# A Fourier-mixing and gated-FFN kernel on one Trainium2 core: a reordered opening, earlier x loads and earlier layer-2 work

## The chip, the cores and the metric

The kernel runs on one core of one Trainium2 chip. The metric is device time in microseconds (us) of one execution. Each timed kernel ran beside the kernel before on the same chip, in the same rounds.

The engines are called by the names that the profile uses: PE (matrix multiplication), PEld (its weight loads), ACT (activation functions and copies), DVE (vector work), POOL (a second vector engine, which here also issues some DMAs) and SP (which issues the other DMAs). A "q" behind a name, as in SPq, means the engine's instruction queue, that is the time to issue something. Batches, chunks and blocks are counted from 0.

## The reference

A Fourier transform along the tokens and one along the channels, of which the real part goes into a gated feed-forward layer:

```python
def _attn_ref(x):                       # x: 8 x 3008 x 256, float32
    X = np.fft.fft(x, axis=1)
    X = np.fft.fft(X, axis=2)
    return X.real.astype(np.float32)

def _moe_ref(x, w_gate, w_val, w_out):  # x: 24064 x 256; weights 256x1536, 256x1536, 1536x256
    g = x @ w_gate
    gelu = 0.5 * g * (1.0 + erf(g * inv_sqrt2))
    return (gelu * (x @ w_val) @ w_out).astype(np.float32)
```

## The kernel before

The channel transform is folded into the two first-layer weights. The token transform is done in two stages of matmuls, after "folds" that add and subtract x and a mirrored copy of x; the mirrored copy comes by a gather (a DMA with an index for each row). Tokens are handled in pairs, t and 3008 minus t, so each batch has three chunks of up to 512 pairs.

The main work is cut into **blocks**: one block is 128 hidden units of one chunk, 12 blocks a chunk, 36 a batch, 288 in all. A block has five layer-1 matmuls (gate and value), two gelus on ACT, three multiplications on DVE and one on POOL (the product called h). The 24 layer-2 pieces of a chunk (four matmuls of 128x256 each) are issued two a block, one chunk later. Everything else is attached to block numbers: a table `fill` says which transform step, load, or store follows which block.

```python
    def feed():
        ...                                     # cut: list of all blocks, list of layer-2 works
        for i, (parts, fc) in enumerate(blocks):
            if fc == 0 and i:
                pend = list(works[i // NFC - 1])     # the 24 layer-2 pieces of the chunk before
            parts["G"][fc]()                         # gate, layer 1
            ...
            parts["V"][fc]()                         # value, layer 1
            if pend:
                pend.pop(0)()                        # one layer-2 piece
            for f in pool.pop(i, []):                # folds on POOL
                f()
            ...
            if pend:
                pend.pop(0)()                        # another
            for f in fill.pop(i, []):                # transforms, loads, stores of this block
                f()
```

For batches 2 to 7 the result of the first transform stage is written to scratch memory and read back transposed, as Z. The read is issued by SP, behind whatever SP has queued, and PE's first use of Z is fixed to a block some four blocks later:

```python
            for i, (jg, piece) in enumerate(((2, 1), (1, 2), (0, 3), (3, 4))):
                ...                                  # s: block of the last first-stage step
                if i == 3:
                    at(fill, s + 1, z_write(b, 12, 4))
            at(fill, s + 3, z_read(b))
            items = []
            for gi in range(NG):
                items += [tp_y(b, gi), tp_e(b, gi), tp_o(b, gi)]
            spread(b, items, s + 7, s0 + NS - 3)     # first use of Z at block s + 7
```

The opening, before block 0: POOL makes constants and indices, then issues the gathers and the weight loads; PE is kept busy with dummy matmuls, `warm(n)`, called warm-ups below, which are meant to keep its clock up until the real work comes.

```python
    def opening():
        ...
        pool_consts(); pool_consts2(); index_consts(0)
        cast_mirror(0, 9, 8)                         # first gather of x
        cast_forward(0, 1, 8); cast_mirror(0, 5, 4); cast_mirror(0, 1, 4)
        index_consts(1); cast_mirror(0, 0, 1)
        ...                                          # weight loads
        warm(11)
        vec_consts(); g_phases(); vec_fills(); cw_phases()
        g_sin(9, 7); g_sin_ends(); g_sin(1, 8); cw_sin()
        t_columns(); t_phases(); t_sin()
        warm(10)
        ...
        fold_piece(9, 4); stage1(2)
        warm(4)
        ...                                          # further folds, stages, warm-ups; first weights
```

## Time and profile before

The median is 633.83 us in three runs (633.27 to 634.46).

| stage (times from the span's start) | from, us | to, us | what fills it |
|---|---|---|---|
| opening | 0 | 20.47 | constants, gather, folds, first transform |
| first chunk, 12 blocks without layer 2 | 20.47 | 44.86 | ACT, then DVE, are nearly full |
| second chunk, 12 blocks with layer 2 | 44.86 | 74.18 | PE 97%, POOL full for a while |
| the rest, 264 blocks | 74.18 | 632.1 | PE |

These are lines of the page of the kernel before: the span; busy time and instruction count of each engine; the DMA queue that carries instruction fetches (packets, MB, share of the time of 16 DMA engines); and the chain of work that ended last, by engine.

```profile
span 632.1 us, 13032 instructions
PE 618.9 (98%) x4285; PEld 407.4 (64%) x4285; DVE 580.9 (92%) x937; ACT 432.7 (68%) x855; POOL 505.7 (80%) x511
q8 instruction: 33, 0.54, 0.3%
PE 87%; DMA 4%; DVE 3%; POOL 2%; ACT 2%; issue 1%; POOLq 0%; DVEq 0%; ACTq 0%
```

PE is the limit: it stands for only 13 us of 632. The same is seen stage by stage in the view of busy time in given stretches. Its columns are the stretch, its length, then busy us and instruction count of each engine, the mean granted PE clock, the busy share of the DMA engines, and GB/s:

```profile
core 0: us, PE busy (x) PEld busy (x) DVE busy (x) ACT busy (x) POOL busy (x), PEclk, DMA share, GB/s
20.00:45.00 25.00, 22.45 (x128) 10.37 (x128) 21.25 (x35) 21.34 (x45) 17.51 (x19) 1.00 0.76 121
45.00:75.00 30.00, 29.22 (x231) 19.54 (x230) 26.89 (x42) 21.91 (x44) 25.28 (x27) 1.00 0.42 109
400.00:500.00 100.00, 100.00 (x690) 66.86 (x689) 95.49 (x147) 69.67 (x136) 83.54 (x83) 1.00 0.33 87
```

From 400 to 500 us PE is busy all the time. The chain of work in the opening hangs on the first gather (start, duration, what):

```profile
4.26 5.73 DMA xb<-in_x_dram,idx
```

In the timeline of SP (start, duration, engine, line, operation, out<-in, count) four output stores are issued, and then the read of Z of batch 4. In the timeline of PE the first matmul that uses Z (L574) starts 4.7 us after the read was issued, and in the view of waits between 110 and 632 us (total, times, longest) that matmul waits for Z only 0.5 us in all:

```profile
282.37 2.40 SPq L616 DMA_DIRECT2D out_dram<-out_sb  x4
284.88 0.52 SPq L530 DMA_DIRECT2D Z_sb<-z  x1
```

```profile
288.94 0.60 PE L695 MATMUL ps_o<-Wo_sb,h_sb 128*128 128x256 bf16 x4
289.59 0.22 PE L574 MATMUL ps_dft<-TP,Z_sb 128*4 128x128 bf16 x1
```

```profile
PE ps_dft L574 <- DMA Z_sb<-z: 0.5, 2, 0.2
```

### The profile page before, as it was taken

Reading aid. Unit: us, or ns where it says so; the run is one execution under the profiler, and the core shown is the slowest. Engines: PE = TensorE matmul, PEld = TensorE weight load, DVE = VectorE, ACT = ScalarE, POOL = GpSimd, SP = SyncE. Lnnn points to the kernel's source line nnn. Section 1 sums busy time; section 2 is a strip of 40 time slices with the busy share of each in tenths; the row PEclk is TensorE's granted clock in tenths of the full one; section 3 lists DMA queues with packets and bytes.
Section 4 is the critical chain, followed back from the end, with each engine's and each line's share of the span. In section 5 each row is a group of like instructions: output and inputs, shape, how many; then the busy total and the mean of one; then the engine's idle time right before and its main releaser. Section 6 shows DMA issues by size and latency. Waiting matters only on the chain.

```text
span 632.1 us, 13032 instructions
## 1 busy us (share of the span) xinstructions
PE 618.9 (98%) x4285; PEld 407.4 (64%) x4285; DVE 580.9 (92%) x937; ACT 432.7 (68%) x855; POOL 505.7 (80%) x511
## 2 busy tenths in 40 slices
PE   7999999999999999999999999999999999999997
PEld 3446666666666666666666666666666666666666
DVE  7698889999899989999999999999999999999992
ACT  6787777666766667666776767766776766666651
POOL 8599799989997998879998799968988555555651
PEclk8999999999999999999999999999999999999999
DMA  8931925535454352633635325633222232221123
GB/s 152 179 61 26 250 63 147 139 99 138 121 146 107 91 140 65 167 84 100 156 93 155 93 66 138 153 92 104 57 53 57 75 104 54 52 51 38 43 51 80
DMA packets 51994, 63.84 MB, mean 101 GB/s; under 512 B 7783, under 2 KB 47194, under 8 KB 49530
## 3 DMA queue, kind: packets, MB, share of 16 engines
q1 hardware_dynamic: 45238, 47.23, 28.9%
q0 software_dynamic: 6096, 15.29, 11.5%
q8 instruction: 33, 0.54, 0.3%
q10 hardware_dynamic: 592, 0.49, 0.3%
q14 instruction: 35, 0.29, 0.1%
HBM read 38.86 MB, written 29.38 MB: 108 GB/s over the span
## 4 chain that ended last, share of the span: by engine, by line
PE 87%; DMA 4%; DVE 3%; POOL 2%; ACT 2%; issue 1%; POOLq 0%; DVEq 0%; ACTq 0%
PE ps_o L695 36%; PE ps_g L622 27%; PE ps_v L622 17%; DMA Z_sb<-z 3%; PE ps_dft L508 2%; PE ps_dft L544 2%; POOL h_sb L671 1%; DVE v_sb L669 1%; DMA xb<-in_x_dram,idx 1%; DVE h_sb L667 1%; PE ps_o L757 1%; PE ps_dft L574 1%; ACT gelu_sb L638 1%; DVE ve_sb L656 1%; PE ps_g L695 0%
## 5 line engine op out<-in xcount | busy, mean ns | idle before, releaser
L671 POOL TENSOR_TENSOR h_sb<-gelu_sb,v_sb 128x512 bf16<-128x512 bf16 (+1 forms) x288 | 328.7, 1144 | 106.3 <-DVE v_sb L669 92.0
L695 PE MATMUL ps_o<-Wo_sb,h_sb 128*128 128x256 bf16 (+1 forms) x2232 | 334.9, 273 | 1.0 <-POOL h_sb L671 1.0
L695 PEld LDWEIGHTS <-h_sb 128*128 128x128 bf16 (+1 forms) x2304 | 228.8, 100 | 112.5 <-POOL h_sb L671 2.7
L656 DVE SCALAR_TENSOR_TENSOR ve_sb<-EB_sb,yw,ps_v 128x512 f32<-128x512 bf16 (+1 forms) x288 | 212.1, 737 | 32.8 <-PE ps_v L622 29.0
L638 ACT ACTIVATE gelu_sb<-ps_g 128x512 bf16<-128x512 f32 (+1 forms) x288 | 169.6, 589 | 96.4 <-PE ps_g L622 93.0
L622 PE MATMUL ps_g<-EO_sb,W_sb 128*128 128x512 bf16 (+1 forms) x864 | 231.2, 375 | 2.7 <-ACT gelu_sb L647 2.0
L622 PE MATMUL ps_v<-EO_sb,W_sb 128*128 128x512 bf16 (+1 forms) x576 | 214.4, 375 | 0.5 <-ACT W_sb L423 0.5
L667 DVE TENSOR_TENSOR h_sb<-gelu_sb,ps_v 128x512 bf16<-128x512 bf16 (+1 forms) x288 | 195.0, 677 | 1.1 <-ACT gelu_sb L647 0.7
L669 DVE SCALAR_TENSOR_TENSOR v_sb<-ve_sb,ps_v 128x512 f32<-128x512 f32 (+1 forms) x288 | 192.6, 669 | 0.0
L622 PEld LDWEIGHTS <-W_sb 128*128 128x128 bf16 x1440 | 136.8, 98 | 82.3 <-issue 4.2
L647 ACT ACTIVATE gelu_sb<-ps_g 128x512 bf16<-128x512 f32 (+1 forms) x288 | 169.1, 587 | 0.0
L714 ACT ACTIVATE out_sb<-ps_o 128x512 f32<-128x512 f32 x92 | 54.9, 597 | 36.1 <-PE ps_o L695 36.0
L224 POOL TENSOR_TENSOR eo_sb<-ab_sb 94x512 bf16<-94x512 f32 (+1 forms) x60 | 66.6, 1110 | 0.1
L554 ACT ACTIVATE EO_sb<-ps_dft 128x512 bf16<-128x512 f32 (+1 forms) x44 | 26.0, 590 | 22.5 <-PE ps_dft L544 20.5
L511 ACT ACTIVATE S_sb<-ps_dft 96x512 bf16<-96x512 f32 x48 | 28.2, 587 | 11.3 <-PE ps_dft L508 11.3
L217 POOL TENSOR_TENSOR ab_sb<-x_raw,x_raw 94x508 f32<-94x508 f32 (+1 forms) x30 | 33.0, 1101 | 0.0
L220 POOL TENSOR_TENSOR ab_sb<-x_raw,x_raw 94x508 f32<-94x508 f32 (+1 forms) x30 | 32.9, 1096 | 0.0
L158 POOL DMA_INDIRECT x_raw<-in_x_dram,idx x18 | 17.0, 945 | 2.8 <-issue 0.6
L508 PE MATMUL ps_dft<-eo_sb,G 94*96 94x256 bf16 x102 | 19.2, 274 | 0.0
L544 PE MATMUL ps_dft<-TP,Z_sb 128*128 128x128 bf16 (+1 forms) x188 | 18.2, 218 | 0.5 <-DVE Z_sb L496 0.5
L544 PEld LDWEIGHTS <-Z_sb 128*128 128x128 bf16 x192 | 14.5, 98 | 2.4 <-DVE Z_sb L496 0.7
L757 PE MATMUL ps_o<-gelu_sb 128*128 128x512 bf16 x32 | 11.1, 498 | 1.2 <-DVE col L305 1.2
(128 smaller groups left out, 173.5 us busy)
## 6 DMA issues: line engine op xcount, KB each, us to landing
out_dram<-out_sb SPq DMA_DIRECT2D x361, 64.0 KB
x_raw<-in_x_dram SPq DMA_DIRECT2D x10, 768.0 KB
Z_sb<-z SPq DMA_DIRECT2D x6, 768.0 KB
z<-S_sb SPq DMA_DIRECT2D x6, 576.0 KB
EB_sb<-yrow SPq DMA_DIRECT2D x14, 128.0 KB
x_raw<-in_x_dram SPq DMA_DIRECT2D x2, 640.0 KB
z<-S_sb SPq DMA_DIRECT2D x6, 192.0 KB
EB_sb<-yrow SPq DMA_DIRECT2D x7, 120.2 KB
```

The source lines that it names most:

```text
L217: eng.tensor_tensor(ab(0, 1, up), fwd(1, up), mir(255, down), op=ALU.add)
L224: eng.tensor_tensor(_sub(eo, [[C, nj], [1, 128]], j0 * C + g * 128), ab(0, 0, [[1, 128]]), ab(1, 0, [[1, 128]]), op=op)
L544: nc.tensor.matmul(ps[:, o : o + n], st["Z"][:, pair, g * 128 : g * 128 + 128], _sub(TP, [[1, n]], g * 128), start=True, stop=True)
L622: nc.tensor.matmul(ps[:, :n], W[nm, part][:, fs], src, start=start, stop=stop, **kw)
L638: nc.scalar.activation(gl[:, 0, :n], pg[:, :n], AF.Gelu)
L647: nc.scalar.activation(_sub(gl, [[-1, n]], TOK + n - 1), pg[:, :n], AF.Gelu)
L656: nc.vector.scalar_tensor_tensor(ve[:, :n], EB_bufs[b][:, c0 : c0 + n], yw[:, fc : fc + 1], pv[:, :n], op0=ALU.mult, op1=ALU.add)
L667: nc.vector.tensor_tensor(st["h"][:, fc, 0, :n], gl[:, 0, :n], pv[:, :n], op=ALU.mult)
L669: nc.vector.scalar_tensor_tensor(_sub(vv, [[-1, n]], n - 1), ve[:, :n], 2.0, pv[:, :n], op0=ALU.mult, op1=ALU.subtract)
L671: nc.gpsimd.tensor_tensor(st["h"][:, fc, 1, :n], gl[:, 1, :n], vv[:, :n], op=ALU.mult)
L695: nc.tensor.matmul(pso[:m, half], st["h"][:, fc, sign, h0 : h0 + m], Wo_sb[:, fc, :], start=(fc == 0), stop=(fc == NFC - 1),)
L714: nc.scalar.activation(_sub(osb, [[1, 2 * C]], 0, part_num=m), pso[:m, :], AF.Copy)
```

## The change

Its intent: shorten the opening and use the slack of the first chunk. (1) The first gather goes ahead of all but the first few constants on POOL. (2) The phases of the transform table are computed on half the columns, the rest follows by symmetry; several small operations move between ACT and DVE; the table columns come before the sines. (3) More PSUM tags (sets of matmul output buffers) in the opening, other warm-ups: 23, 7 + 6 + 8 + 2, in place of 32, 11 + 10 + 4 + 2 + 3 + 2. (4) The six casting loads of x of batch 1 are issued in one run in the opening instead of one a block. (5) Six layer-2 pieces move ahead: of the 24 pieces of chunk 0, four are done inside chunk 0 and two in blocks 13 and 14, in place of the regular two a block. (6) The forward part of x of batch 2 is loaded ten blocks sooner. Besides, the weights are loaded in other pieces, and the folds of batch 1 on POOL are attached to other blocks.

```diff
     def index_consts(i):
         idx, base = ((idx_x, NP - 1), (idx_0, NP))[i]
-        nc.gpsimd.iota(col_i[:, i : i + 1], pattern=[[0, 1]], base=base, channel_multiplier=-1, **IOTA)
+        nc.gpsimd.memset(idx, 0)
+        nc.gpsimd.iota(idx[:NP, :], pattern=[[0, 1]], base=base, channel_multiplier=-1)
         ...
-        nc.gpsimd.tensor_scalar(idx, col_i[:, i : i + 1], 0.0, None, op0=ALU.max)
 ... (cut: pool_consts, g_phases, cw_phases, identities, t_columns and others regrouped)
         pool_consts()
-        pool_consts2()
         index_consts(0)
         cast_mirror(0, 9, 8)
+        pool_consts2()
+        cast_mirror(0, 5, 4)
         cast_forward(0, 1, 8)
-        cast_mirror(0, 5, 4)
 ...
+        xb[1] = xb_tile(1)
+        cast_forward(1, 9, 8)
+        cast_mirror(1, 9, 8)
+        cast_forward(1, 0, 9)
+        for j0, nj in ((5, 4), (1, 4), (0, 1)):
+            cast_mirror(1, j0, nj)
 ...
-        warm(11)
         vec_consts()
+        vec_fills()
+        warm(7)
         g_phases()
-        vec_fills()
-        cw_phases()
-        g_sin(9, 7)
-        g_sin_ends()
-        g_sin(1, 8)
-        cw_sin()
         t_columns()
         t_phases()
+        g_rows(9, 7)
+        t_reduced()
+        vec_consts2()
+        identities()
+        cw_phases()
 ...
-        warm(10)
+        warm(6)
+        fold_piece(9, 4)
+        s1(0, 2, 0)()
+        s1(0, 2, 1)()
+        warm(8)
 ...
-        for s, f in (
-                (0, second_x), (1, lambda: cast_mirror(1, 9, 8)), (2, lambda: cast_forward(1, 0, 9)),
-                (3, lambda: cast_mirror(1, 5, 4)), (4, lambda: cast_mirror(1, 1, 4)),
-                (5, lambda: cast_mirror(1, 0, 1))):
-            at(fill, s, f)
 ...
-        slot_of = [6 + i * 13 // len(ops) for i in range(len(ops))]
+        slot_of = [6, 7, 8, 9, 10, 14, 15, 16, 17, 18]
 ...
+        for k, s in ((0, 8), (1, 9), (2, 9)):
+            at(fill, s, lambda k=k: load_part(2, k, (load_forward,)))
         for k, s in ((0, 18), (1, 19), (2, 19)):
-            at(fill, s, lambda k=k: load_part(2, k))
+            at(fill, s, lambda k=k: load_part(2, k, (load_mirror,)))
 ...
+        first = works[0]
+        sooner = {6: [first[0]], 7: [first[3]], 10: [first[1]], 11: [first[4]], 13: [first[2]], 14: [first[5]]}
+        works[0] = first[6:]
 ...
+            two = sooner.pop(i, []) if i <= NFC + 2 else [pend.pop(0) for _ in range(2) if pend]
```

## The prediction

> **What bounds the kernel now.** From about 75 us on, the tensor engine: in the table of stretches PE is busy 99 to 100%, and the chain of waits is 87% PE. One block (128 hidden units, one chunk of tokens) takes about 2.1 us. The change leaves this alone, so it wins only in the first 75 us; what it wins should stay, as the later schedule counts blocks, not time.
>
> Three stages lie before that, read from the timelines (batches counted from 0):
> - Opening: first layer-1 matmul at 20.47 us, its second half at 21.11. Chain: index constants on POOL until 3.98, gather of x from 4.26 to its landing at 9.99, folds on DVE, copies on ACT. ACT starts the stage-1 copies only at 13.42; sines, table load and constants hold it till then.
> - First chunk, to 44.9: 24.4 us for 12 blocks, no layer 2. ACT is nearly full from 25 to 35 (weight copies), DVE without a gap from 31.7 to 52.7 at 1.86 us a block; PE idles about 2.5 us.
> - Second chunk, to 74.2: 29.3 us, 2.44 us a block, with all 24 layer-2 pieces of the first. POOL is full from 40 to 55; PE stands 0.63 us for POOL's h, DVE 1.0 us for PE.
>
> **The change, costed.**
> 1. Gather sooner: the 0.55 us index cast, two iotas and one of 1.38 us leave the queue ahead of it; it issues near 1.9 instead of 4.26. Sharing the DMA with the staging load (until about 5.9), I estimate landing near 8.
> 2. Folded phases: 816-wide ops (0.58, 1.00 us) and a 0.72 us add become about 400-wide. But the moved iota now ends near 5.2 and DVE waits for it in mid-phase; DVE also takes the identities, the rest of CW and the TP write. I estimate the first fold at 9.3, not 10.02. ACT starts the copies about 0.7 us sooner. The Trainium skill ("ScalarE: Activation LUTs", Table sets) says that copy, identity and abs are in every set, so no third table load; the trace before agrees with two loads of 1.28 us.
> 3. More PSUM tags, fewer warm-ups before the last part: 0.5 to 1 us. The opening in sum: first gate near 18.7, gain 1.8 us (0.5 to 3).
> 4. Casts of batch 1 in one run: about 5 us of POOL issue time leave the first chunk. DVE limits there, so directly 0.3 us; less lateness of POOL at 50 to 55 gives 0.5.
> 5. Four layer-2 pieces (0.435 us each) go into the first chunk's PE slack: 1.7 us; calmer first blocks of chunk two: 0.3.
> 6. Forward x of batch 2 sooner: POOL idles 1.8 us before its first fold at 75.97, PE loses 0.3 at 80 to 85: 0.2.
>
> Sum 4.8 us, nearly all on the chain of waits: **629.0 us**, range **625.5 to 632.0**. Chances: faster by over 2% 0.03, within 2% 0.96, slower 0.01.
>
> **What would show it.** First layer-1 matmul at 18 to 19.5; first chunk 23.5 to 24.4 us long; second 26.5 to 27.5; then the same pitch to the end. POOL no longer full at 45 to 55.
>
> **What would make it wrong.** The DMA is over 90% busy for most of 8 to 33 us: if weights land late, blocks 2 to 6 wait. The PE clock, 0.69 at 10 to 15 us, could stay low with fewer warm-ups. Layer-2 pieces could make PE wait for POOL's h in the first chunk. Or ACT's order could hold the stage-1 copies where they are, which costs item 2 whole.

## The result, and the profile after

In four runs each, before took 633.72 us (633.27 to 634.46) and after 633.73 us (633.38 to 634.22). The ratio is 1.000, with a 95% interval of 0.9982 to 1.0017. Ratios here and below are the mean time of one kernel's runs over that of the other's of the same rounds, so they are not quite the ratio of the medians. The result is correct. It lies within 2%, as the prediction thought most likely, but above its range of 625.5 to 632.0.

The same lines of the page, after:

```profile
span 631.7 us, 13013 instructions
PE 615.7 (97%) x4276; PEld 406.3 (64%) x4276; DVE 579.5 (92%) x942; ACT 432.9 (69%) x852; POOL 503.3 (80%) x508
q8 instruction: 33, 0.54, 0.4%
PE 84%; DMA 7%; POOL 4%; DVE 2%; issue 1%; ACT 1%; SPq 0%; POOLq 0%; ACTq 0%; DVEq 0%
```

PE has 3.2 us less to do, and the span is 0.4 us shorter. The chain now has 7% of DMA where it had 4%. Note a small thing that will matter: PE has 9 matmuls and 9 weight loads, that is 18 instructions, fewer. The stretches, after:

```profile
20.00:45.00 25.00, 23.12 (x139) 11.67 (x139) 21.75 (x35) 21.40 (x45) 17.24 (x18) 1.00 0.87 162
45.00:75.00 30.00, 29.44 (x230) 19.36 (x229) 28.02 (x44) 23.25 (x47) 27.61 (x31) 1.00 0.34 90
400.00:500.00 100.00, 99.54 (x685) 66.45 (x684) 95.16 (x147) 69.03 (x134) 82.52 (x83) 1.00 0.33 87
```

In the first 75 us PE gets more done, as hoped. From 400 to 500 us, where nothing was changed, it is no longer at 100.00.

Where the gain came and went is best seen from the start of each block, read in both traces as the start of its first gelu (after minus before, us):

| block | 0 | 11 | 24 | 36 | 126 | 130 | 166 | 202 | 238 | end |
|---|---|---|---|---|---|---|---|---|---|---|
| difference | -1.65 | -0.73 | -3.00 | -3.00 | -3.25 | -2.25 | -1.60 | -1.07 | -0.41 | -0.47 |

So the change did win 3.25 us (3.00 by block 36, the other 0.25 at blocks 66 and 100, which was not looked into), and the kernel then lost 2.84 us of it in four steps, one a batch, each where Z of batches 4 to 7 is first used (blocks 127, 163, 199 and 235, a little before those batches begin). Between the steps the two kernels run at the same pitch to 0.01 us. The place is the read of Z. In SP's timeline of after, the four stores ahead of the read of batch 4 take 3.45 us where they took 2.40, and the read is issued later by as much:

```profile
279.12 3.45 SPq L644 DMA_DIRECT2D out_dram<-out_sb  x4
282.68 0.52 SPq L558 DMA_DIRECT2D Z_sb<-z  x1
```

In PE's timeline the first use of Z (now L602) stands for 1.05 us, in brackets: idle time, and what ended it. From issue to use it takes 4.65 us, no longer than before. The view of waits after 110 us has 3.4 us where it had 0.5:

```profile
285.68 0.60 PE L724 MATMUL ps_o<-Wo_sb,h_sb 128*128 128x256 bf16 x4
287.33 0.22 PE L602 MATMUL ps_dft<-TP,Z_sb 128*4 128x128 bf16 x1 [1.05 <-DMA Z_sb<-z]
```

```profile
PE ps_dft L602 <- DMA Z_sb<-z: 3.4, 5, 1.1
```

Summed over all six reads in the trace, PE's idle time at that matmul is 0.60 us before and 3.42 after. The difference of 2.82 us accounts for the loss of 2.84. (The read of batch 3 also has a slow store ahead of it, of 1.53 us, but its first use comes 5.6 us after the issue, so that nothing waits.)

Why did the stores take longer? One of the four issues takes 1.63 us instead of 0.59. It starts at 280.29. The view of DMA for the stretch 280 to 282 us shows, beside the packets of the data queue q1, one packet of q8, a queue that the profile marks as instruction fetches, as it does q14 (the first line is the busy share of the DMA engines in 40 slices of 0.05 us, in tenths):

```profile
DMA  0009053958653000005585892200001010010101
q1 hardware_dynamic: 156, 0.13, 27.0%
q8 instruction: 1, 0.02, 4.3%
```

The trace has that packet at 280.16, of 16,384 bytes, with 1.38 us; it is under way when the slow store issue starts. The packets are slower too: over the whole execution one takes 0.98 us in the median before and 1.24 after. The packets of q14, of 8,192 bytes, don't explain the stores: none is under way during any of the four slow ones ahead of the reads of batches 4 to 7. Over the whole execution q8 has 33 such packets. I take them for PE's own instructions, for three reasons. Their size is that of 256 instructions by the page named below, and 33 times 256 is 8,448, close to the 8,552 instructions of PE and PEld on the page. They come every 18.5 us on average; 256 instructions of PE take 18.9 us at the mean pitch of the whole span. And each of them starts when the count of PE instructions begun, taken modulo 256, is between 158 and 198, apart from two of the first five. The Trainium skill ("Runtime: NRT & Kernel Launch", Instruction fetch mechanics) says that an engine's instruction memory is refilled in blocks of 16 KiB, 256 instructions, by a DMA queue of the sequencer's own; size and number in this trace agree. It adds that the cost of crossing a boundary is "mostly hidden". PE's own stream shows no cost here either (before, PE is busy for 100.00 of 100 us from 400 us on, with five fetches in that time); but SP's stores do:

| output-store issues, of 376 | touch a q8 fetch | of these over 0.75 us | touch none | of these over 0.75 us |
|---|---|---|---|---|
| before | 11 | 4 | 365 | 4 |
| after | 33 | 16 | 343 | 6 |

There is a last piece, which explains why the loss comes in each batch: in the middle batches one batch has exactly 1,024 PE instructions (counted in the trace from block 108 to 144, and so on), which is four times 256. So the fetches come at the same place of every batch. Before, one starts 4.0 to 4.2 us ahead of each Z read of batches 4 to 7, which is before the four stores begin; after, it starts 1.9 to 2.5 us ahead, in the midst of them. At the mean pitch 18 instructions are 1.3 us. Against the first of the four stores the fetch moved by 2.6 to 3.1 us. The other half is in the count itself: these four fetches begin some 20 PE instructions later in the count after than before. Why they do is not shown; the count fixes a fetch only to within some 40 instructions.

In the opening and the first chunk, other things were not as predicted. The timeline of POOL after, from 15 to 32 us:

```profile
18.46 0.52 POOL L179 DMA_DIRECT2D xb<-in_x_dram  x1 [0.51 <-DMA w_raw<-in_moe_w_gate_dram]
23.11 0.95 POOL L158 DMA_INDIRECT xb<-in_x_dram,idx  x1 [4.13 <-DMA w_raw<-in_moe_w_val_dram]
27.52 0.92 POOL L158 DMA_INDIRECT xb<-in_x_dram,idx  x1 [3.45 <-DMA w_raw<-in_moe_w_gate_dram]
29.66 3.41 POOL L699 TENSOR_TENSOR h_sb<-gelu_sb,v_sb 128x512 bf16<-128x512 bf16 x3
```

Before, POOL's first h product was at 26.30. After, POOL stands 4.13 and 3.45 us ahead of two gathers of batch 1 and begins h at 29.66. What it waits for are earlier weight loads: as the trace's semaphores show, POOL's DMAs share eight semaphores of this program in rotation, and each waits for the landing of the one eight before it. Issued one a block, that wait was over by the time; issued in one run, it holds POOL up.

### The profile page after: what moved, and what is told of

The parts are those of the page before. It is cut to its first block, busy times and chain, and to the rows that moved or that the text cites. A ratio compares the mean times of both kernels' runs of the same rounds, so it can differ in the third digit from the quotient of the medians.

```text
span 631.7 us, 13013 instructions
## 1 busy us (share of the span) xinstructions
PE 615.7 (97%) x4276; PEld 406.3 (64%) x4276; DVE 579.5 (92%) x942; ACT 432.9 (69%) x852; POOL 503.3 (80%) x508
## 4 chain that ended last, share of the span: by engine, by line
PE 84%; DMA 7%; POOL 4%; DVE 2%; issue 1%; ACT 1%; SPq 0%; POOLq 0%; ACTq 0%; DVEq 0%
PE ps_o L724 35%; PE ps_g L650 26%; PE ps_v L650 17%; DMA Z_sb<-z 4%; DMA w_raw<-in_moe_w_gate_dram 2%; POOL h_sb L699 2%; PE ps_dft L536 2%; PE ps_dft L572 1%; DVE v_sb L697 1%; POOL xb L158 1%; DMA EO_sb<-yrow 1%; POOL w_raw L422 1%; PE ps_dft L602 1%; PE ps_dft L517 1%; PE ps_g L724 0%
## 5 line engine op out<-in xcount | busy, mean ns | idle before, releaser
L158 POOL DMA_INDIRECT xb<-in_x_dram,idx x8 | 7.7, 965 | 9.2 <-DMA w_raw<-in_moe_w_val_dram 4.1
```

## The experiments

Twelve kernels ran, all with correct results. The first four were sent together, then the next four, then the last four; the kernel before ran beside each call with medians of 633.52, 634.15 and 633.33 us, 11 runs each. The three calls ran on three chips, so kernels of different calls are best compared by their ratios.

### Is it the instruction fetch? Only the number of PE instructions is changed

The theory: the place of PE's fetches against the blocks decides whether the store issues ahead of the Z read are slow. The rivals: something else that the change brought, such as other DMA traffic, delays the Z read; or PE simply reaches Z sooner than the DMAs can deliver it. The expectations call the theory F and the last rival P (pace). The first experiment leaves the change whole and cuts nine warm-up matmuls into two of half the width, which restores the 18 PE instructions for the same work:

```diff
             for _ in range(n):
-                nc.tensor.matmul(ps[:, :], idle[:, 0:128], idle[:, :], start=True, stop=True)
+                w = 256 if split[0] > 0 else 512        # split starts at [9]
+                split[0] -= 1
+                for c in range(0, 512, w):
+                    nc.tensor.matmul(ps[:, c : c + w], idle[:, 0:128], idle[:, c : c + w], start=True, stop=True)
```

> The changed kernel, with nine of its warm-up matmuls cut into two halves of 256 columns: the same PE work, 18 more PE instructions, so 8553 as in the kernel before instead of 8535. Theory F (fetch): the changed kernel loses 2.6 of its 3.0 us in four waits of PE for the Z read, because a 16384-byte instruction fetch of PE now falls on the output stores that are issued just ahead of that read (one store took 1.63 us instead of 0.59 at 280.3 us, the fetch began at 280.2). With the fetches back at their old places the four waits (1.05, 0.87, 0.46, 0.75 us) fall to 0.25 or less and the time to about 631.1 us. Theory P (pace): PE now simply reaches the Z read sooner than the DMA chain can deliver; then the waits stay at 0.5 to 1.05 us and the time at 633.7.

Measured: 630.68 us (629.80 to 632.44, six runs), ratio 0.9959 [0.9947, 0.9972]. SP's timeline has the stores at 2.40 us again, and PE's first use of Z comes without a wait:

```profile
279.47 2.40 SPq L644 DMA_DIRECT2D out_dram<-out_sb  x4
281.98 0.52 SPq L558 DMA_DIRECT2D Z_sb<-z  x1
```

```profile
286.56 0.22 PE L602 MATMUL ps_dft<-TP,Z_sb 128*4 128x128 bf16 x1
```

The fetches start 4.1 to 4.25 us ahead of the Z reads, as before, and again 11 store issues touch one. A change of nine dummy matmuls at the start of the kernel brings 3 us at 280 to 510 us. That is what the theory says, and the rivals cannot, for the DMA traffic is that of after and the pace nearly so (2.9 us ahead of before at block 126, after 3.25).

The second experiment is the converse: the kernel *before*, with nine warm-ups fewer and nothing else.

```diff
-        warm(11)
+        warm(6)
 ...
-        warm(10)
+        warm(6)
```

> The kernel before, with nine warm-up matmuls fewer in the opening (6 and 6 instead of 11 and 10), so 18 PE instructions fewer, 8535 as in the changed kernel. Theory F: its steady state then has the fetches on the same stores as the changed kernel, so the waits for Z at the starts of batches 4 to 7 grow from 0.0 to 0.2 us each to 0.5 to 1.05 us, and the time grows by about 2.6 us to 636.3. Theory P: no gain in pace was made, so no waits: 633.7 us, or less if the warm-ups were in the way (they are on the chain of the opening for part of 11.8 to 14.3 us, but not these).

Measured: 637.68 us (637.43 to 638.64, five runs), ratio 1.0071 [1.0058, 1.0084]: slower by 4.2 us. In the view of waits after 110 us the Z wait of this kernel grows from 0.5 us to 3.3:

```profile
PE ps_dft L574 <- DMA Z_sb<-z: 3.3, 4, 0.9
```

It has no gain in pace, so theory P falls here too: its opening is as long as before (first gelu at 21.59 instead of 21.52). 35 store issues touch a fetch. The Z waits explain 2.7 us; another 1.3 us is lost at block 27, where POOL waits 3.1 us, as I read it for the late x of batch 2: its gather landed at 77.24 us and the fold began at 77.31, though the profile names a DVE product that ended as late (compare the run on the forward loads below).

### Giving the read more slack

The third experiment takes the wait away without touching the instruction count: the Z read is issued one block sooner, for batches 4 to 7 ahead of the stores instead of behind them. In the trace it waits for the same semaphore as after's, and the results are correct. The fourth makes the same edit to the kernel before.

```diff
-            at(fill, s + 3, z_read(b))
+            at(fill, s + 2, z_read(b))
```

> The changed kernel with the Z read queued one block (about 2.1 us) sooner, ahead of four output stores instead of behind them; PE program the same. Theory F: the stall of the stores no longer delays the read, Z has landed before it is used, all waits for Z go, and the time is about 631.0 us. Theory P, if what limits is the rate of the DMA chain itself (write of Z, then read): the read waits for the landing of the write, the data come no sooner, 633.7.

> The kernel before with the same earlier Z read. Its six waits for Z sum to 0.6 us only, so both theories expect 633.1 us, the same within noise. If it gains 2 us or more, the waits for Z cost more in the kernel before than its trace shows, and F's account of what was lost is incomplete.

Measured: on after, 629.89 us (629.08 to 630.38, five runs), ratio 0.9945 [0.9933, 0.9958]; on before, 633.65 us (632.67 to 636.77, six runs), ratio 1.0010 [0.9993, 1.0027]. Neither trace has a Z wait left. In c's SP timeline the read of batch 4 goes first, and the stores behind it are still slow, but nobody waits for them:

```profile
277.36 0.34 SPq L558 DMA_DIRECT2D Z_sb<-z  x1
278.13 6.33 SPq L644 DMA_DIRECT2D out_dram<-out_sb  x5
```

So the edit is worth 3.5 us to after by the ratios (3.8 by the medians) and nothing measurable to before: the wait is what kept the change from paying, and the change itself is worth about 3.5 us. All further experiments are built on this version, called c below, so that the fetches do not blur them.

### What each part is worth

Three of the prediction's terms could be undone alone: the casts in one run, the earlier layer-2 pieces and the earlier forward loads. The times of all these kernels lie close together, so the stages are compared as read from the profiles, in us. Stage lengths are from the first gelu of one block to that of another; the middle stages repeat from profile to profile within a few hundredths where the DMA doesn't disturb them, while the opening does not repeat.

| kernel | first gelu | blocks 1 to 11 | 11 to 24 | 24 to 36 |
|---|---|---|---|---|
| before | 21.52 | 19.53 | 31.40 | 26.81 |
| after | 19.87 | 20.69 | 29.13 | 26.81 |
| c: after, Z read sooner | 20.22 | 20.16 | 29.13 | 26.82 |
| e: c, three casts back in blocks 3 to 5 | 19.83 | 20.16 | 29.54 | 26.81 |
| f: c, layer-2 pieces back | 21.45 | 19.53 | 30.10 | 26.82 |
| g: c, both back | 21.75 | 19.53 | 30.10 | 26.82 |
| h: c, forward loads back | 19.50 | 20.16 | 29.13 | 28.30 |
| i: c, pieces at other blocks | 20.22 | 19.83 | 29.46 | 26.82 |
| j: c, columns later | 19.25 | 22.46 | 29.12 | 26.82 |
| k: j, shorter warm-ups | 20.78 | 20.16 | 29.13 | 26.82 |
| l: i and k | 20.66 | 19.87 | 29.46 | 26.82 |

**The casts.** The last three gathers of batch 1 go back to one a block:

```diff
-        for j0, nj in ((5, 4), (1, 4), (0, 1)):
-            cast_mirror(1, j0, nj)
 ...
+        for s, f in (
+                (3, lambda: cast_mirror(1, 5, 4)), (4, lambda: cast_mirror(1, 1, 4)),
+                (5, lambda: cast_mirror(1, 0, 1))):
+            at(fill, s, f)
```

> The changed kernel with the early Z read (so that the end is not blurred by those waits), and with the last three gathers of batch 1 put back between POOL's first products. In the changed kernel POOL stood 4.1 and 3.5 us for weight loads to land before it might issue two of these gathers (each POOL DMA waits for the landing of the eighth before it), and its first h came at 29.66 us, 3.4 us later than before, though the gate ran 1.9 us ahead. Theory Q (queue): that lateness costs most of the 0.6 us that are lost between blocks 1 and 11 (1.53 ahead of before at block 1, 0.90 at block 11); with the gathers back the first h comes near 24.5 us, block 11 runs 1.4 or more ahead, and the time falls by 0.5 us to about 629.4. Theory L (layer 2): the loss comes from the four layer-2 pieces now done in this chunk, then nothing moves at block 11, and the time stays 629.9.

Measured: 630.31 us (629.45 to 631.72), ratio 0.9943 [0.9931, 0.9955], the same as c. POOL begins h at 24.33, where after begins at 29.66 and c at 29.42:

```profile
24.33 1.16 POOL L699 TENSOR_TENSOR h_sb<-gelu_sb,v_sb 128x512 bf16<-128x512 bf16 x1 [5.48 <-DVE v_sb L697]
```

But blocks 1 to 11 take 20.16 us in both e and c, and blocks 11 to 24 take 0.41 us less with the casts in one run. So POOL's late start did not cost c anything, and theory Q of the expectation, that POOL's waits lengthen the first chunk, does not hold for c. In after's own profile it did cost 0.53 us (20.69 instead of 20.16, at block 5, where a gelu waited for POOL's h), and in j it cost 2.3 us. Whether it costs anything depends on when the weights land, against the blocks, in that execution.

**The layer-2 pieces.**

```diff
-        sooner = {6: [first[0]], 7: [first[3]], 10: [first[1]], 11: [first[4]], 13: [first[2]], 14: [first[5]]}
-        works[0] = first[6:]
+        sooner = {}
 ...
-            two = sooner.pop(i, []) if i <= NFC + 2 else [pend.pop(0) for _ in range(2) if pend]
+            two = sooner.pop(i, []) if i < NFC else [pend.pop(0) for _ in range(2) if pend]
```

> The changed kernel with the early Z read, and all 24 layer-2 pieces of the first chunk back in the second chunk. Both theories expect the second chunk to be longer by about 1.7 us (four pieces of 0.435 us). Theory L: the first chunk then keeps the whole lead, 1.5 us at block 11, so that the net loss at block 36 is about 1.1 us: 631.0 us. Theory Q: block 11 stays near 0.9 ahead and the loss is the full 1.7 us: 631.6.

Measured: 630.44 us (629.62 to 632.30), ratio 0.9945 [0.9931, 0.9958]. Sooner pieces cost 0.63 us in blocks 1 to 11 and win 0.97 in blocks 11 to 24: net 0.34 us. The prediction had 2.0. The reason, as the traces suggest it: PE does not set the pace there. DVE has no idle time from block 5 to 13 in f, and from block 5 to 16 only 0.21 us in c; where another engine is full, PE work that moves ahead cannot shorten the whole. These are after's stretches, in which DVE (the third of the busy times) is busy 5.00 of 5 us each time:

```profile
45.00:50.00 5.00, 4.59 (x31) 2.52 (x29) 5.00 (x9) 4.11 (x8) 5.00 (x6) 1.00 0.00 0
50.00:55.00 5.00, 4.85 (x41) 3.19 (x42) 5.00 (x9) 3.38 (x7) 4.90 (x7) 1.00 0.21 52
```

The rest of the second chunk's gain over before, 31.40 to 30.10, stays in f, so it does not come from the pieces; a wait of 0.63 us that PE had for POOL's h at 52.77 us is gone there, with the folds of batch 1 regrouped over the blocks, but that was not tested alone.

**Both back.** The edits of e and f together, to see whether they add up.

> The two edits before this one together: the casts and layer 2 as in the kernel before; the opening and the earlier forward load of batch 2 stay. If the effects simply add, the lead at block 36 is the opening's 1.5 us and little more, and the time about 631.5 us. If the casts in one run pay only together with layer 2 in the first chunk, the time is that of f_l2_later or less.

Measured: 630.19 us (629.38 to 631.72, five runs), ratio 0.9934 [0.9921, 0.9947]. Its stages are those of f. The casts make no difference once the pieces are late. Its profile happened to be its slowest run.

**The forward loads of batch 2.**

```diff
-        for k, s in ((0, 8), (1, 9), (2, 9)):
-            at(fill, s, lambda k=k: load_part(2, k, (load_forward,)))
         for k, s in ((0, 18), (1, 19), (2, 19)):
-            at(fill, s, lambda k=k: load_part(2, k, (load_mirror,)))
+            at(fill, s, lambda k=k: load_part(2, k))
```

> The changed kernel with the early Z read, and the forward x of batch 2 loaded where it was before (blocks 18 and 19 instead of 8 and 9). The prediction gave this part 0.2 us. In b_rows_less POOL stood 3.1 us before its first fold of batch 2, and PE lost 1.27 us at block 27, so the part may be worth up to 1.3 us when the load is unlucky: expected 630.1 us if the prediction is right, up to 631.2 if not; the lead at block 26 stays 3.2 us and falls at block 27.

Measured: 631.51 us (630.51 to 632.83), ratio 0.9963 [0.9949, 0.9976]. In its profile POOL waits for x, and five microseconds later PE waits for POOL (the first line from POOL's timeline, the second from PE's):

```profile
73.56 0.22 POOL L215 TENSOR_TENSOR ab_sb<-x_raw,x_raw 94x8 f32<-94x8 f32 x1 [3.31 <-DMA x_raw<-in_x_dram,idx]
```

```profile
78.50 0.28 PE L724 MATMUL ps_o<-Wo_sb,h_sb 128*128 128x256 bf16 x1 [1.31 <-POOL h_sb L699]
```

Blocks 24 to 36 take 1.48 us longer. The kernel before has its loads just as late and takes 26.81 us; there they landed in time. So this part of the change shows no gain in before against after, yet without it c's profile is 1.5 us worse; the totals agree in direction, though their intervals overlap. It is insurance against a late landing.

### Can it be made better?

Three more edits, from what the runs above showed. The first moves three of the early pieces out of blocks 7, 10 and 11, which the expectation takes for full on PE:

```diff
-        sooner = {6: [first[0]], 7: [first[3]], 10: [first[1]], 11: [first[4]], 13: [first[2]], 14: [first[5]]}
+        sooner = {6: [first[0]], 8: [first[3]], 9: [first[1]], 12: [first[4]], 13: [first[2]], 14: [first[5]]}
```

> The changed kernel with the early Z read, and the sooner layer-2 pieces moved from blocks 7, 10 and 11, where PE already had a weight or column piece and the block grew by 0.3 to 0.4 us, to blocks 8, 9 and 12. If full PE blocks are why layer 2 in the first chunk cost 0.63 us there (e_casts_later has ruled out POOL's lateness), the loss from block 1 to block 11 falls from 0.63 to 0.2 us or less, and the lead from block 1 to block 36 grows from 1.64 to about 2.0 us. If DVE limits that chunk whatever PE does, the loss stays. The total, about 629.5 us, will not tell it apart; the trace must.

Measured: 630.31 us (629.38 to 631.56), ratio 0.9949 [0.9935, 0.9963]. The first chunk loses 0.30 us instead of 0.63, and the second gains that much less. The sum from block 1 to 24 is 49.29 us in both. Moving pieces among those blocks moves the time from one chunk to the other, and doesn't change the sum. So full PE blocks are not why the pieces won so little; it fits DVE's setting the pace.

The second came from the opening. Ten small matmuls that turn rows into table columns sit on DVE's path to the first fold. In after's profile they take 1.24 us, in c, f and g 2.26, and the first fold is at 8.61 or at 9.85 (both lines are from PE's timeline, the first of after, the second of f):

```profile
4.40 1.24 PE L389 MATMUL ps_v<-one,par 1*128 1x1 f32 x10 [0.19 <-DVE par L287]
```

```profile
4.40 2.26 PE L389 MATMUL ps_v<-one,par 1*128 1x1 f32 x10
```

The PE clock makes the difference: the first change in the trace's clock record, to full speed, stands at 3.88 us in after and at 15.43 in f. (Before its first change the record is empty and PEclk reads 1.00 all the same, so go by the matmuls' durations there.) The warm-ups next to them show it too: eight of them took 3.61 us in f, 0.45 us each, and 1.89 us in c, 0.24 each. The Trainium skill ("TensorE: Matmul & The Clock Gate", Part 1: The HAM clock gate) gives 427 and 216 ns for such matmuls at the half and the full clock, says that the clock is raised after some 3.4 us of work, and that the window in which the work is counted runs free, so that the moment differs from run to run. The figures here agree: from start to start these warm-ups are 427 ns apart in f and 216 in c. So does the spread of the opening over executions of nearly the same code: 19.50 to 21.75 us to the first gelu in after, c, e, f, g and h.

The opening of the kernel before spreads as well: its first gelu is at 20.41 us in d, where the clock is full from 6.25 us on, and at 21.52 in before, where it is at half from 11.94 to 15.35. Compared in like states of the clock, the new opening is 1.65 us sooner (after against before), 0.91 (h against d), or not sooner (f and g against b, which has nine warm-ups less; full from 15.0 to 16.0 us on in all three). So the 1.65 us are of one pair of profiles, and what the opening wins on the average is not known.

In f and g the slow warm-ups moreover held the next stage of PE back until 14.97 and 14.99 us, and ACT's copies stood 1.39 us for it. So two edits were tried: the columns behind the first table rows, off the path (j), and in addition the eight warm-ups at half width (k).

```diff
-        t_columns()
-        t_phases()
         g_rows(9, 7)
-        t_reduced()
         vec_consts2()
         identities()
         cw_phases()
+        t_columns()
+        t_phases()
+        t_reduced()
 ...
-        warm(8)
+        warm(8, 256)     # in k and l only
```

> The changed kernel with the early Z read; ACT and DVE do the G rows, the identities and the CW phases before what depends on the ten small table-column matmuls (PE program the same). In ten profiles so far the first gelu of the same opening came anywhere from 19.50 to 21.75 us, and the column matmuls took 1.24 us or 2.26 us, by the clock of PE. If their wait on the chain is what spreads the opening, the first fold starts at 8.9 us or sooner in every profile, not at 8.6 to 9.9, and the first gelu at 20.3 or sooner if PE is not cold again afterwards; median about 629.3. If the spread comes from elsewhere, the first gelu can still come after 21 us.

> As j_columns, and the eight warm-up matmuls behind the first stage-1 pair cut to 256 columns each, so that they take half the time and the same number of instructions. In the two slow openings these eight ran at half clock, 3.6 us, and held the second stage-1 pair until 15.0 us, while its fold was done at 14.1. Expected: the second pair's copies start by 13.8 us in any clock state, first gelu at 19.8 or sooner, median about 628.9. If the shorter warm-up lets the clock fall, later matmuls slow down and the gain is gone: 629.9 or more.

> All of these together: early Z read, moved pieces, columns later, shorter warm-up. If the gains add: 628.5 us, a ratio of 0.992 to the kernel before.

Measured: j 629.80 us (628.99 to 630.78), ratio 0.9938 [0.9925, 0.9951]; k 630.12 us (629.43 to 631.57), 0.9948 [0.9933, 0.9962]; l, which is k with the pieces of i, 629.99 us (629.76 to 633.80), 0.9954 [0.9932, 0.9975]. In j the edit did what it was made for: the columns took 2.26 us, and the first fold was at 8.65 all the same, the first gelu at 19.25. But its POOL had the worst waits of all, and a gelu on ACT stood for it (the first two lines are from POOL's timeline, the last from ACT's):

```profile
21.41 0.95 POOL L158 DMA_INDIRECT xb<-in_x_dram,idx  x1 [2.59 <-DMA w_raw<-in_moe_w_val_dram]
28.68 0.92 POOL L158 DMA_INDIRECT xb<-in_x_dram,idx  x1 [6.31 <-DMA w_raw<-in_moe_w_gate_dram]
```

```profile
32.03 0.60 ACT L666 ACTIVATE gelu_sb<-ps_g 128x512 bf16<-128x512 f32 x1 [1.35 <-POOL h_sb L699]
```

In k and l the clock was low: from 12.4 to about 18 us the real matmuls ran at half speed (five of the first stage took 0.61 us where after needs 0.38), and the first gelu was at 20.78 and 20.66. In after and e, with full-width warm-ups, the clock also fell near 11 us but was back at 14.12 and 14.67, against 18.14 and 17.70 in k and l. So the warm-ups seem to have been of use; two profiles each don't prove it. None of e, f, g, i, j, k and l can be told from c by its time. All of them, like c and a, beat both the kernel before and the kernel after. The best that these runs support is c, for it is the smallest edit.

## Why the prediction was wrong

*"What it wins there should stay, as the later schedule counts blocks, not time."* **This is the step that failed.** The blocks do keep their pitch, but the instruction fetches don't follow blocks. They follow, to within some 40, the count of PE instructions from the start, and the change has 18 fewer of them. So the fetches fell onto the stores ahead of the Z reads, and 2.84 us of 3.25 were lost. That is shown from both sides: 18 instructions back on after give 630.68 us, 18 taken from before give 637.68, and a read issued one block sooner takes the wait away and gives 629.89. I had read "PE 100%" in the later stretches as slack enough for the rest; I had not looked at how close to its use each DMA landed.

The terms of the sum were wrong in size as well, and would have left a lead of 3.0 us at block 36 instead of 4.8:

- **1, the gather.** Right in kind: it was issued at 1.91 us (predicted near 1.9), and the first fold came at 8.61 in after's profile, better than the 9.3 predicted. But it came at 9.85 in the profiles where the columns ran at the low clock.
- **2, the phases.** The moved index constant was priced at its old 1.38 us and was to end near 5.2. With its new pattern it ended at 3.58. ACT began the copies 1.34 us sooner in after, not 0.7, but only 0.11 sooner in c and f, where the columns ran at the low clock. As predicted with the Trainium skill ("ScalarE: Activation LUTs", Table sets), no third table load appeared: the trace after has two again, of 1.28 us.
- **3, the opening in sum.** Predicted 1.8 us (0.5 to 3), measured 1.65 at the first gelu (the first layer-1 matmul came at 19.01, inside the predicted 18 to 19.5). The same opening gave anything from 2.02 us sooner than before (h) to 0.23 later (g), by the state of the clock. The opening of the kernel before moved by 1.11 us itself, so that part of the 1.65 may be luck. The prediction named this risk, but gave it no width.
- **4, the casts in one run.** Predicted a gain of 0.8 us. Measured: 0.41 gained where the weights land in time, 0.53 lost in after's profile, 2.3 lost in j's. What was overlooked is the wait for the eighth DMA before. POOL was also still full at 45 to 55 us (5.00 and 4.90 of 5 us in the two halves), against the prediction.
- **5, the layer-2 pieces.** Predicted 2.0 us, measured 0.34. They were counted as if filling PE's slack in the first chunk shortened the whole, but by the traces DVE sets the pace there; the prediction itself has DVE without a gap from 31.7 to 52.7 us. Moving three of the pieces (i) left the sum of both chunks at 49.29 us. The first chunk became 25.1 us long, not 23.5 to 24.4. The second was 27.3, inside the 26.5 to 27.5 predicted, but for the most part for another reason.
- **6, the forward loads.** Predicted 0.2. Before against after it is nothing to be seen; without it the quicker kernel c lost 1.5 us in its profile.

Still open: why an instruction fetch of 16 KiB holds up the issue of a store on another queue. The Trainium skill ("DMA: Bandwidth & Descriptors", Issuing engines are not separate DMA queues) says that DMAs issued by different engines run on the same 16 DMA engines and interleave. A slow issue alongside a fetch would fit that, if the fetch runs there too, but what inside the DMA hardware holds the issue up was not measured. And not each issue that touches a fetch is slow: 16 of 33 were.

## What to carry to other kernels

A saving at the start of a tuned kernel lasts to the end only if each later DMA lands with room to spare, so look at the waits of the first consumer of every transfer, and move a transfer with no margin forward before you judge anything else. A change that adds or removes a few instructions on the busiest engine can shift its instruction fetches for the rest of the program; here nine dummy matmuls moved the time by three to four us, as much as the change under study is worth, so try a small change at two instruction counts before you believe its time. And price work that is moved into slack from the particular slots where it goes, not from a stage's total of idle time, and ask first which engine sets the pace there.

## What the Trainium skill lacked or had wrong

- "Runtime: NRT & Kernel Launch", Instruction fetch mechanics: that crossing a 16 KiB boundary is "mostly hidden" doesn't hold for the other engines' DMAs. A PE fetch of 16,384 bytes took 1.38 us in the trace after, and a store issue on SP beside it took 1.63 us instead of 0.59. Of 33 store issues that touched a fetch, 16 took over 0.75 us; of 343 that touched none, 6 did.
- The same page doesn't spell out that the fetches recur in step with a regular program: a batch has 1,024 PE instructions here, four blocks of 256, so one fetch met the same read in batch after batch, and 18 PE instructions put back on after made it about 3 us faster, while 18 taken from before made it 4.2 us slower.
- "TensorE: Matmul & The Clock Gate" was right about the free-running window: the clock record's first change to full speed comes anywhere from 3.88 to 16.02 us in these traces. But it has no figure for very small float32 matmuls: ten of 1x1 took 1.24 us at one clock and 2.26 us at the other.
- No page has it: in this program a DMA issued on POOL waits for the landing of the eighth one before it, and POOL stood 4.13 and 3.45 us for weight loads when gathers were issued in one run (6.31 us in one experiment).
